# Turning the row maxima of an attention kernel by a DMA transpose instead of a TensorE product, and moving two staging slots

## The chip, the cores and the metric

The kernel runs on one core of one Trainium2 chip. The metric is the device time of one execution in microseconds. Before the change the median of three runs is 1665.59 us (1664.72 to 1666.26).

## The reference

One transformer block on a sequence of 2048 rows of width 512 (float32), with a modulation that a vector `c` sets:

```python
mod = (_silu(c) @ w_mod).reshape(c.shape[0], 6, 1, -1)
sa, ca, ga, sb, cb, gb = (mod[:, 0], ..., mod[:, 5])
h = _layernorm(x) * (1 + ca) + sa
x = x + ga * _A_ref(h, A_wq, A_wk, A_wv, A_wo)
h = _layernorm(x) * (1 + cb) + sb
x = x + gb * _B_ref(h, B_w_gate, B_w_up, B_w_down)
```

`_A_ref` is attention with 32 query heads of width 16 that share one key and one value head. `_B_ref` is a gated layer without a nonlinearity, `((h @ w_gate) * (h @ w_up)) @ w_down`, with 1792 inner columns. What matters here is the softmax over 2048 keys, `softmax(q k^T / 4)`, for each head and each query row.

## The kernel before

**Units.** The attention is done in 32 units. A unit `u` is 256 query rows (`ST`) of 8 heads, held as two halves `a`, each of four heads in pairs. Its queries lie in one of three buffers, `sst[u % 3]`, with the head's numbers on partitions 0 to 47 and 64 to 111. For a unit the kernel needs the row maximum of each of its 2048 (head, row) pairs before it may take exponentials. So there is a **maximum pass** over the scores, one unit ahead, and then the pass proper:

- `max_mm` (the product is L601) multiplies 128 query rows with 512 keys, and VectorE reduces the 128x512 product to one column of `mpart` (L605). Four such pairs stand in each turn of the main loop.
- When all of a unit's parts are there, `max_fin` (L622) reduces `mpart` to `mm`, 128 partitions x 16 columns: the query row lies on the partition, the half and head on the column.
- `max_rows` turns `mm`, since the pass proper wants the maxima as two further rows of the queries' buffer, partitions 48, 49 (and 112, 113): then one product yields the score minus its row's maximum. The maximum is held as a sum of two float16 numbers.
- `qk_exp` makes scores with the keys on partitions (L657 and L659, 50 rows deep: 48 and the two rows of maxima), and ScalarE takes the exponential into a tile `P` (L661).
- `pv` (L670) multiplies `P` with the values, eight products in a group, one turn later.

**The main loop.** `attend(u, kt)` writes two turns at a time, 16 turns to a unit, by a fixed pattern of score products, maximum products and "side" products (L511). The side products are the query projection in the first units, and then the output projection and the gated layer of rows that are finished. The pool of PSUM banks is a queue of eight; a tile that is "held" keeps its bank until it is given back. The kernel is under a manual schedule: what stands in an engine's queue, and in what order, is the order in which this code records it.

**Posts and timers.** `drain_posts()` runs at the start and in the middle of each turn and records what was put off: functions in `posts`, and those that `after(delay, f)` set for that many calls later.

**Turning the maxima before.** When a unit's last part is recorded, `max_rows(u)` gives two functions. The first (`f`, run by `late_max()` one step of the maximum pass later) holds a PSUM bank and lets TensorE multiply `mm` with the identity (L629, `mxt`). The second (`g`, at the next `drain_posts()`) lets ScalarE write the high half from PSUM to float16, scaled by 1/32 (L634, `mt`), lets VectorE write the rest (L635), and issues from SyncE one DMA of 2 x 8 x 128 numbers for each half into the two rows of `sst[u % 3]` (L639).

**The work that the SyncE queue carries.** Every DMA of the main loop is issued by SyncE (SP) in the order of recording: reloading queries (`load_q`, L566), saving and reloading a unit's outputs and their sums (L679, L686, L690, L695, L700), input rows and results (L733, L866), and the weights that come late (L937).

**Staging the late weights.** `stage(n)` loads one slice of a weight (448 or 512 columns of float32) into the next of the six slots of `SLOTS`, round and round. The slots are pieces of one large buffer, `kwb`, 14 slots long. While column norms are formed, the sums of squares lie in the same buffer: `ssqs[0]` from slot 4 on, 1792 columns (to the middle of slot 7), `ssqs[1]` the same length from slot 8 on. GpSimd squares a slice in its slot (L944) and adds it to those sums (L946). Slots 6 and 7 are thus used both for slices and for part of `ssqs[0]`.

Of the kernel before, what the change touches and what calls it, by code (L numbers as in the profile page):

```python
# [13 lines left out]
F32 = mybir.dt.float32  # L14
F16 = mybir.dt.float16
# [16 lines left out]
SQ_GAP = 2.6  # L32
LAG = 2
ROW_LAG = 4
SLOTS = (0, 1, 2, 3, 6, 7)
SUM_GAP = 4.0
SUM_LAG = 3
SPLIT_GAP = 2.5
# [25 lines left out]
def adaln_mqa_glu_kernel(ctx: ExitStack, tc: tile.TileContext, x_in, wq_in, wk_in, wv_in, wo_in,  # L64
# [159 lines left out]
    kwb = big.tile([128, 2 * FT * D], F16, name="kwb", tag="wd")  # L224
    hfs = kwb[:, 0:2 * NHF * BT].bitcast(F32).rearrange("p (n t) -> p n t", n=NHF)
    ssqs = [kwb[:, 2 * n * BT:2 * n * BT + 2 * F].bitcast(F32) for n in (KC, 2 * KC)]
    kng = kwb[:, 2 * NHF * BT:2 * NHF * BT + BT]

    def hf(b, k):
# [390 lines left out]
    def max_fin(u):  # L620
        mms[u] = work.tile([128, 2, 8], F32, name="mm")
        nc.vector.tensor_reduce(mms[u], mparts[u], axis=AX.X, op=OP.max)  # L622

    def max_rows(u):
        def f():
            mms[u, "b"] = ps_hold("mxt")
            p = mms[u, "b"][0:16, 0:128]
            mms[u, "p"] = p
            nc.tensor.transpose(p, mms[u].rearrange("p a c -> p (a c)"), ident)  # L629

        def g():
            p = mms[u, "p"]
            mt = [work.tile([16, 128], F16, name=f"mt{hl}") for hl in range(2)]
            nc.scalar.activation(mt[0], p, AF.Copy, scale=1.0 / 32.0)  # L634
            nc.vector.scalar_tensor_tensor(mt[1], p, 1.0 / 32.0, mt[0], op0=OP.mult, op1=OP.subtract)  # L635
            ps_give(mms[u, "b"])
            s = sst[u % 3]
            for hl in range(2):
                nc.sync.dma_start(s[48 + hl:113 + hl:64].rearrange("p c q n -> p (c q n)"), mt[hl])  # L639
        return [(100, f, g)]  # L640

    pvb = {}
    ptl = {}
# [249 lines left out]
    def late_weights():  # L893
# [37 lines left out]
        def stage(n):  # L931
            if "d" in W:
                t = work.tile([128, D], F32, name="wsl", tag="xl", bufs=3)
            else:
                t = hfs[:, SLOTS[taken[0] % len(SLOTS)], :]
                taken[0] += 1
            nc.sync.dma_start(t[:, :sl[n][3]], sl[n][2])  # L937
            st[n] = t
# [174 lines left out]

    wlist, dlist, mod_rows = late_weights()
    NSTEP = 32
    later = {}
    mstep = [0, 0]

    def drain_posts():
# [8 lines left out]
    def max_half(a):  # L1128
        n = mstep[a]
        mstep[a] += 1  # L1130
        if n >= len(flat):
            return
        u, i, last, ops = flat[n]
        max_parts(u)
        for kind, p, t, kc in ops[a]:
            max_mm(u, a, (kind, p, t, kc))
        if mstep[1 - a] <= n:
            return
        u, i, last, ops = flat[n]
        if 0 < u < NU - 1 and i == QPRE:  # L1140
            load_q(u + 1)
        if i == 12:
            max_parts(u + 1)
        if last:
            max_fin(u)
            (_, f, g), = max_rows(u)
            later[min(mstep) + 1] = (f, g)

    def late_max():
        for at in [m for m in later if m <= min(mstep)]:  # L1150
            f, g = later.pop(at)
            f()
            posts.append(g)
            return True
        return False

# [25 lines left out]
    qs = deque(q_proj(b, ch) for b in range(NB) for ch in ((2, 3, 0, 1) if b == 0 else range(KC)))  # L1184
    for n in range(LEAD):
        drain_posts()
        late_max()
        for _ in range(1 if n >= PAIRED else 2 - 2 * (n % 2)):
            max_half(0)
            max_half(1)  # L1190
# [27 lines left out]
    def attend(u, kt):  # L1218
# [10 lines left out]
        def end_turn(kt):  # L1229
# [7 lines left out]
            if v >= 0:  # L1237
                pv(*divmod(v, KT))
                if v % KT == KT - 1:
                    ends.append(lambda: pv_out(u - 1))  # L1240
            if not late_max() and turns and all(q.ended() for q in qs):
                _, f, post = turns.popleft()
                f()
                posts.append(post)
            hooks(u, 2 * kt + 1)

        for turn in range(2):
# [4 lines left out]
            for j, (what, a) in enumerate(order):  # L1252
                if j == len(order) // 2:
                    drain_posts()
                    if style is not NO_SIDE:
                        late_max()
                    hooks(u, 2 * (kt + turn))
                a = a if style is NO_SIDE else a ^ turn
                if what == "m" and mstep[a] >= len(flat) and style is MANY:
# [117 lines left out]
```

## Time and profile before

| what | us |
|---|---|
| median of three runs | 1665.59 |
| span of the profiled execution (first to last instruction) | 1663.8 |
| PE busy in it | 1643.3 |
| DVE busy | 1402.3 |
| ACT busy | 1234.8 |
| POOL busy | 523.5 |

The profiled execution's span leaves out what lies before the first and behind the last instruction; against the median of the runs that is 1.8 us. The profile calls TensorE's products PE and its weight loads PEld, VectorE DVE, ScalarE ACT, GpSimd POOL and the issuing of SyncE's DMAs SPq. In a timeline the columns are start (us), duration (us), engine, line, operation, output<-inputs, shapes, how many instructions the row joins, and in brackets the idle time of the engine before it with what ended it. In a group the numbers behind the bar are the busy time in us and the mean ns of one. Until 76 us the inputs are prepared; then unit 0 begins, and a unit takes some 41 to 49 us. The last unit's scores begin at 1505 us, and from 1551 us only the gated layer of the last rows is left.

### The profile page before, as it was taken

What the parts mean: (1) busy time and instruction counts of PE and PEld (TensorE: products, weight loads), DVE (VectorE), ACT (ScalarE), POOL (GpSimd) and SP (SyncE); (2) the same over time, 40 slices, a digit from 0 to 9 for tenths busy, and PEclk for the clock granted to TensorE, in tenths of its full rate; (3) what the DMA queues carried; (4) which work ended last, traced back from release to release, by engine and by line L of the source; (5) the groups of instructions that cost most, each with busy time, mean ns of one, the idle gap of its engine ahead of it and who ended that gap; (6) DMA issues with size and microseconds to landing.
All of it is one profiled execution on the core that took longest, in us unless ns stands there. A gap on an engine that the chain in (4) does not pass through costs nothing.

```text
span 1663.8 us, 39821 instructions
## 1 busy us (share of the span) xinstructions
PE 1643.3 (99%) x15677; PEld 747.1 (45%) x15677; DVE 1402.3 (84%) x2434; ACT 1234.8 (74%) x2389; POOL 523.5 (31%) x833
## 2 busy tenths in 40 slices
PE   8899999999999999999999999999999999999999
PEld 4333333355533554335543355434545345454776
DVE  7999999998998999899998999999998999980211
ACT  5688888888777877777877787777878777877300
POOL 4857537864841111301112011300113001210322
PEclk9999999999999999999999999999999999999999
DMA  6313313342210001000000000000000000000100
GB/s 237 108 59 100 95 43 120 96 129 80 77 51 24 18 12 32 19 32 20 20 26 23 25 13 24 26 25 26 20 29 15 26 22 20 26 14 21 33 13 14
DMA packets 66024, 75.39 MB, mean 45 GB/s; under 512 B 17702, under 2 KB 46634, under 8 KB 65836
## 3 DMA queue, kind: packets, MB, share of 16 engines
q1 hardware_dynamic: 63724, 72.26, 13.7%
q8 instruction: 123, 2.02, 0.5%
q10 hardware_dynamic: 2112, 0.59, 0.1%
q14 instruction: 65, 0.53, 0.1%
HBM read 55.51 MB, written 17.04 MB: 44 GB/s over the span
## 4 chain that ended last, share of the span: by engine, by line
PE 93%; ACT 2%; DVE 2%; DMA 1%; issue 1%; POOL 0%; SPq 0%; ACTq 0%; DVEq 0%
PE side L511 41%; PE pv L670 30%; PE mx L601 8%; PE sc L659 8%; PE sc L657 3%; ACT P L661 2%; DVE mpart L605 1%; DMA xbig<-in_A_x_dram 1%; PE mx L805 1%; PE mxt L629 0%; ACT hf L813 0%; PE sc L601 0%; DVE bs L248 0%; DMA kwb<-in_B_w_down_dram 0%; DMA wkv<-in_A_wv_dram 0%
## 5 line engine op out<-in xcount | busy, mean ns | idle before, releaser
L605 DVE TENSOR_REDUCE mpart<-mx 128x1 f32<-128x512 f32 x2016 | 1274.1, 684 | 104.0 <-PE mx L601 95.7
L661 ACT ACTIVATE P<-sc 128x512 f32<-128x512 f32 x2048 | 1094.8, 598 | 274.2 <-PE sc L659 226.9
L601 PE MATMUL mx<-kst,sst 48*128 48x512 f16 x2032 | 631.5, 377 | 3.8 <-ACT P L661 1.7
L659 PE MATMUL sc<-sst,kst 50*128 50x512 f16 x1792 | 597.5, 379 | 0.6 <-ACT P L661 0.3
L670 PE MATMUL pv<-P,vst 128*32 128x512 f32 x4096 | 545.3, 605 | 0.7
L511 PE MATMUL side<-h2T,wg 64*128 64x256 f16 (+1 forms) x2396 | 540.8, 271 | 0.1
L511 PE MATMUL side<-h2T,wu 64*128 64x256 f16 (+1 forms) x2396 | 538.7, 270 | 0.0
L511 PEld LDWEIGHTS <-wg 64*128 64x128 f16 (+1 forms) x2396 | 226.0, 94 | 230.5 <-ACT P L661 194.0
L511 PE MATMUL side<-wd,glu 64*128 64x512 f16 (+1 forms) x1172 | 272.8, 378 | 0.2 <-ACT P L661 0.2
L850 POOL TENSOR_SCALAR glu<-gf 128x256 f16<-128x256 f32 x112 | 45.8, 409 | 671.3 <-DVE gf L849 583.9
L511 PEld LDWEIGHTS <-wu 64*128 64x128 f16 (+1 forms) x2396 | 226.4, 94 | 43.0 <-issue 7.8
L601 PEld LDWEIGHTS <-sst 48*128 48x128 f16 x2064 | 189.9, 94 | 34.2 <-issue 17.4
L659 PEld LDWEIGHTS <-kst 50*128 50x128 f16 x1792 | 162.9, 94 | 63.0 <-issue 50.3
L511 PEld LDWEIGHTS <-glu 64*128 64x128 f16 (+1 forms) x1172 | 98.5, 94 | 192.4 <-ACT P L661 85.9
L670 PEld LDWEIGHTS pv<-P,vst 128*32 128x32 f32 x4096 | 80.7, 108 | 160.9 <-issue 150.1
L849 DVE TENSOR_TENSOR gf<-side,g 128x256 f32<-128x256 f32 x112 | 46.7, 418 | 79.8 <-ACT g L847 77.7
L657 PE MATMUL sc<-sst,kst 50*128 50x256 f16 x512 | 96.9, 268 | 0.1
L511 PE MATMUL side<-h,wq 64*128 64x512 f16 (+1 forms) x372 | 95.0, 376 | 0.4 <-ACT P L661 0.4
L847 ACT ACTIVATE g<-side 128x256 f32<-128x256 f32 x112 | 42.3, 379 | 65.6 <-PE side L511 65.3
L511 PE MATMUL side<-wo,och 64*128 64x512 f16 (+1 forms) x360 | 86.3, 377 | 0.0
L851 POOL TENSOR_TENSOR glu<-gf,glu 128x256 f16<-128x256 f32 x112 | 75.3, 673 | 9.3
L706 POOL TENSOR_TENSOR oc<-oc,rr 128x256 f32<-128x256 f32 x31 | 22.7, 731 | 146.6 <-DMA rr<-ri 100.4
(233 smaller groups left out, 865.4 us busy)
## 6 DMA issues: line engine op xcount, KB each, us to landing
pd<-ev SPq DMA_DIRECT2D x32, 256.0 KB
kwb<-in_B_w_gate_dram SPq DMA_DIRECT2D x32, 224.0 KB
kwb<-in_B_w_up_dram SPq DMA_DIRECT2D x32, 224.0 KB
sst<-qd SPq DMA_DIRECT2D x180, 32.0 KB
qd<-q SPq DMA_DIRECT2D x16, 256.0 KB
oc<-pd SPq DMA_DIRECT2D x64, 64.0 KB
rr<-ri SPq DMA_DIRECT2D x64, 64.0 KB
x<-in_A_x_dram SPq DMA_DIRECT2D x14, 256.0 KB
```

Source lines behind the costliest of these rows:

```text
L511: return nc.tensor.matmul(self.p[:, c * w:(c + 1) * w], left[rows], right[rows], start=start and c == 0, stop=stop and c == len(terms) - 1)
L601: nc.tensor.matmul(m, s[64 * a:64 * a + 48, t // 2, p, t % 2 * 128:(t % 2 + 1) * 128], w[64 * a:64 * a + 48, :], start=(i == 0), stop=(i = ...
L605: nc.vector.tensor_reduce(part, m, axis=AX.X, op=OP.max)
L657: nc.tensor.matmul(t[:, c * ST:(c + 1) * ST], keys, s[64 * a:64 * a + 50, c, p, :], start=True, stop=True)
L659: nc.tensor.matmul(t.rearrange("k (c n) -> k c n", c=2), keys, s[64 * a:64 * a + 50, :, p, :], start=True, stop=True)
L661: ex = nc.scalar.activation(ptl[u, kt, p, a], t, AF.Exp)
L670: nc.tensor.matmul(pvb[u][32 * j:32 * j + 32, :], vst[:, kt, :], ptl[u, kt, p, a], start=(kt == 0), stop=(kt == KT - 1))
L706: eng.tensor_tensor(o, o, st["r"], op=OP.mult)
L847: nc.scalar.activation(g, p[:, 0:ST], AF.Copy, scale=2.0 ** -45)
L849: nc.vector.tensor_tensor(gf, p[:, ST:2 * ST], g, op=OP.mult)
L850: nc.gpsimd.tensor_scalar(glu()[:, 0, f, :], gf, 1.0, 0.0, op0=OP.mult, op1=OP.add)
L851: nc.gpsimd.tensor_tensor(glu()[:, 1, f, :], gf, glu()[:, 0, f, :], op=OP.subtract)
```

## The change

`max_rows` now works on `mm` as it lies. VectorE writes `mm / 32` in float16 into the first 16 columns of a 128x128 float16 tile `mtc` (L632 of the changed kernel) and the rest into the next 16 (L633); the other columns are zeros, which GpSimd writes once at the start. There are two such tiles, used in turn. One `drain_posts()` later, SyncE issues a DMA with `transpose=True` of the whole 128x128 tile into `mtT`; two calls after that it issues the same two DMAs of rows as before, now from 16 partitions each of `mtT`. The product with the identity, its bank, ScalarE's copy, `late_max` and `later` are gone. Since `late_max()` no longer says that it did something, the piece of the main loop that takes work from `turns` no longer steps back for it.

Apart from that, the staging slots are now 0, 1, 2, 3, 12 and 13 of `kwb` instead of 0, 1, 2, 3, 6 and 7.

```diff
-SLOTS = (0, 1, 2, 3, 6, 7)
+ROWS_LAG = 2
+SLOTS = (0, 1, 2, 3, 12, 13)
...
+    stg = kwb.bitcast(F32).rearrange("p (n t) -> p n t", t=BT)
...
+    mtc = consts.tile([128, 2, 128], F16, name="mtc")
+    nc.gpsimd.memset(mtc, 0.0)
+    mtT = consts.tile([128, 2, 128], F16, name="mtT")
+
     def max_rows(u):
-        def f():
-            mms[u, "b"] = ps_hold("mxt")
-            p = mms[u, "b"][0:16, 0:128]
-            mms[u, "p"] = p
-            nc.tensor.transpose(p, mms[u].rearrange("p a c -> p (a c)"), ident)
-
-        def g():
-            p = mms[u, "p"]
-            mt = [work.tile([16, 128], F16, name=f"mt{hl}") for hl in range(2)]
-            nc.scalar.activation(mt[0], p, AF.Copy, scale=1.0 / 32.0)
-            nc.vector.scalar_tensor_tensor(mt[1], p, 1.0 / 32.0, mt[0], op0=OP.mult, op1=OP.subtract)
-            ps_give(mms[u, "b"])
+        m, c = mms[u].rearrange("p a c -> p (a c)"), mtc[:, u % 2, :]
+        nc.vector.tensor_scalar(c[:, 0:16], m, 1.0 / 32.0, None, op0=OP.mult)
+        nc.vector.scalar_tensor_tensor(c[:, 16:32], m, 1.0 / 32.0, c[:, 0:16], op0=OP.mult, op1=OP.subtract)
+        t = mtT[:, u % 2, :]
+
+        def rows():
             s = sst[u % 3]
             for hl in range(2):
-                nc.sync.dma_start(s[48 + hl:113 + hl:64].rearrange("p c q n -> p (c q n)"), mt[hl])
-        return [(100, f, g)]
+                nc.sync.dma_start(s[48 + hl:113 + hl:64].rearrange("p c q n -> p (c q n)"), t[16 * hl:16 * hl + 16, :])
+
+        after(1, lambda: nc.sync.dma_start(t, c, transpose=True))
+        after(1 + ROWS_LAG, rows)
...
-                t = hfs[:, SLOTS[taken[0] % len(SLOTS)], :]
+                t = stg[:, SLOTS[taken[0] % len(SLOTS)], :]
...
-            (_, f, g), = max_rows(u)
-            later[min(mstep) + 1] = (f, g)
+            max_rows(u)
...
-            if not late_max() and turns and all(q.ended() for q in qs):
+            if turns and all(q.ended() for q in qs):
```

The lines of the changed kernel carry numbers that are two higher around here (the product L601 is L603, the reduction L605 is L607).

On TensorE nothing moves but the 32 products with the identity, which go. The queue around the one of unit 3, with the unit's `sst_128` not yet in use (`sst_130` is unit 2's, whose scores are running, `sst_129` unit 4's, whose maxima are being formed). Before:

```order
L601 MATMUL mx<-kst,sst_129 128x512
L670 MATMUL pv<-P,vst 32x512 x4
L629 MATMUL mxt<-ident,mm 16x128
L659 LDWEIGHTS kst
L659 MATMUL sc<-sst_130,kst 128x512
L601 LDWEIGHTS sst_129
L601 MATMUL mx<-kst,sst_129 128x512
```

Now:

```order
L603 MATMUL mx<-kst,sst_129 128x512
L672 MATMUL pv<-P,vst 32x512 x4
L661 LDWEIGHTS kst
L661 MATMUL sc<-sst_130,kst 128x512
L603 LDWEIGHTS sst_129
L603 MATMUL mx<-kst,sst_129 128x512
```

The group of value products is now followed at once by the next turn's score product. In both kernels the first score product of the new unit stands behind the second group of value products after this place, in every unit from 1 on.

On VectorE the work on the maxima moves up to the reduction that makes them. Around unit 19 (`x_11103`, now `x_11064`, are result rows to which the gated layer is added). Before:

```order
L605 TENSOR_REDUCE mpart<-mx 128x1 x29
L622 TENSOR_REDUCE mm<-mpart 128x16
L605 TENSOR_REDUCE mpart<-mx 128x1 x2
L635 SCALAR_TENSOR_TENSOR mt_15689<-mxt,mt_15688 16x128
L605 TENSOR_REDUCE mpart<-mx 128x1 x4
L865 SCALAR_TENSOR_TENSOR x_11103<-side,sca,x_11103 128x512
```

Now:

```order
L607 TENSOR_REDUCE mpart<-mx 128x1 x29
L624 TENSOR_REDUCE mm<-mpart 128x16
L632 TENSOR_SCALAR mtc<-mm 128x16
L633 SCALAR_TENSOR_TENSOR mtc<-mm,mtc 128x16
L607 TENSOR_REDUCE mpart<-mx 128x1 x6
L867 SCALAR_TENSOR_TENSOR x_11064<-side,sca,x_11064 128x512
```

Two operations stand where one stood two reductions later.

On SyncE one DMA is added for each unit, and the two of rows can fall behind others. The queue at the same unit 19 (`sst_129` is its buffer, `out_dram` the store of those result rows, `pd` and `rc` the saved outputs of a unit and the reload of their sums). Before:

```order
L566 DMA sst_130<-qd_0_3023 16x4x256 x6
L639 DMA sst_129<-mt_15688 2x8x128
L639 DMA sst_129<-mt_15689 2x8x128
L866 DMA out_dram<-x_11103 128x512
L679 DMA pd_15891<-ev 128x512
L686 DMA rc<-pd_15891 128x1x16
```

Now:

```order
L568 DMA sst_130<-qd_0_3014 16x4x256 x6
L641 DMA_TRANSPOSE mtT<-mtc 128x128
L868 DMA out_dram<-x_11064 128x512
L639 DMA sst_129<-mtT 2x8x128 x2
L681 DMA pd_15834<-ev 128x512
L688 DMA rc<-pd_15834 128x1x16
```

The rows have fallen behind the store, which waits for VectorE's `x_11064`. It is the only unit where a store has come between. In units 1 to 3, 6 and 7 a load of weights stands between the transpose and the rows, in unit 5 a load of input rows and one of weights; in units 14, 23 and 28 a store that stood ahead of the rows now stands ahead of the transpose, in units 7 and 8 a load of weights that stood behind the rows does so too; in the other units the rows follow the transpose directly.

More of the change, by code (lines that the diff above doesn't have):

```diff
@@ L1115, in adaln_mqa_glu_kernel @@
     NSTEP = 32
-    later = {}
     mstep = [0, 0]
@@ L1145, in max_half @@
             max_fin(u)
-            (_, f, g), = max_rows(u)
-            later[min(mstep) + 1] = (f, g)
[L1149 to L1155, printed above, removed]
+            max_rows(u)
     fill = deque()
@@ L1186, in adaln_mqa_glu_kernel @@
         drain_posts()
-        late_max()
         for _ in range(1 if n >= PAIRED else 2 - 2 * (n % 2)):
@@ L1254, in attend @@
                     drain_posts()
-                    if style is not NO_SIDE:
-                        late_max()
                     hooks(u, 2 * (kt + turn))
```

## Prediction

> **What bounds the kernel now.** I read the page's first lines, then the chain of waits with its shares by line, then the removed tile, and then timelines around single units.
>
> ```profile
> PE 1643.3 (99%) x15677; PEld 747.1 (45%) x15677; DVE 1402.3 (84%) x2434; ACT 1234.8 (74%) x2389; POOL 523.5 (31%) x833
> PE 93%; ACT 2%; DVE 2%; DMA 1%; issue 1%; POOL 0%; SPq 0%; ACTq 0%; DVEq 0%
> by line: PE side L511 41.2%; PE pv L670 29.9%; PE mx L601 8.5%; PE sc L659 8.2%; PE sc L657 2.8%; ACT P L661 1.7%; DVE mpart L605 1.0%; DMA xbig<-in_A_x_dram 0.6%; PE mx L805 0.6%; issue 0.5%; PE mxt L629 0.4%; ACT hf L813 0.4%; PE sc L601
> ```
>
> TensorE is busy for 99% of the span and is 93% of the chain. So what is taken out of its queue shortens the run, unless something else is late in the same turn. The chain holds the products to be removed with 0.4%, which is 0.004 x 1663.8 = 6.7 us.
>
> ```profile
> L629 PE MATMUL mxt<-ident,mm x32: 269/277/278, 68.3 to 1499.5; 128*16 128x128 f32 x32
> L634 ACT ACTIVATE mt<-mxt x32: 250/267/268, 68.6 to 1499.9; 16x128 f16<-16x128 f32 x32
> L635 DVE SCALAR_TENSOR_TENSOR mt<-mxt,mt x32: 267/278/279, 70.5 to 1500.2; 16x128 f16<-16x128 f32 x32
> ```
>
> Products are pipelined, so 277 ns is not yet what one costs. TensorE around unit 27 shows it:
>
> ```profile
> 1308.84 1.06 PE L670 MATMUL pv<-P,vst 128*32 128x512 f32 x8
> 1311.67 1.07 PE L670 MATMUL pv<-P,vst 128*32 128x512 f32 x8
> 1312.67 0.28 PE L629 MATMUL mxt<-ident,mm 128*16 128x128 f32 x1
> 1312.88 0.39 PE L511 MATMUL side<-wd,glu 64*128 64x512 f16 x1
> ...
> 1317.65 1.07 PE L670 MATMUL pv<-P,vst 128*32 128x512 f32 x8
> 1318.65 0.39 PE L511 MATMUL side<-wd,glu 64*128 64x512 f16 x1
> 1318.66 0.39 PE L659 MATMUL sc<-sst,kst 50*128 50x512 f16 x1
> ```
>
> A plain turn is 1311.67 - 1308.84 = 2.83 us. Behind a group of value products the next product starts 1.00 us after the group (1317.65 to 1318.65); with the transpose it starts 1.21 us after it (1311.67 to 1312.88). One transpose costs the queue 0.21 us. The last row is the first score product of unit 27: the second group after the transpose ends there, and this product reads the rows of maxima. That is the deadline of the new route.
>
> **What goes.** TensorE: 32 x 0.21 = 6.7 us, on the bound engine, the same as the chain's share. ScalarE: 32 x 0.267 = 8.5 us, which I cost at nothing, since ScalarE is busy 74%. Their waits go too:
>
> ```profile
> ACT mt L634 <- PE mxt L629: 15.0, 29, 2.9
> DVE mt L635 <- ACT mt L634: 2.6, 5, 1.2
> L605 DVE TENSOR_REDUCE mpart<-mx 128x1 f32<-128x512 f32 x2016 | 1274.1, 684 | 104.0 <-PE mx L601 95.7
> ```
>
> ScalarE stood 15.0 us for the transposes and VectorE 2.6 us for ScalarE. Mostly these hid in time that the engines had spare anyway (VectorE waits 95.7 us for TensorE's products), so I book nothing for them; the bound on the other side is the product's whole 0.277 us and VectorE's waits, 32 x 0.277 + 2.6 = 11.5 us. The freed bank is booked at nothing as well.
>
> **What VectorE gets.** One operation of 278 ns goes, two of 128 x 16 come. Small ones cost it this:
>
> ```profile
> 63.99 0.22 DVE L404 TENSOR_REDUCE evs<-ident 128x1 f32<-128x64 f32 x1
> 64.12 0.15 DVE L405 RECIPROCAL evt<-kb 128x1 f32<-128x1 f32 x1
> 64.19 0.68 DVE L610 CUSTOM_DVE_ANT_0 rel<-mx,rel 128x512 f32<-128x512 f32 x1
> 1313.28 0.28 DVE L635 SCALAR_TENSOR_TENSOR mt<-mxt,mt 16x128 f16<-16x128 f32 x1
> 1313.53 2.56 DVE L605 TENSOR_REDUCE mpart<-mx 128x1 f32<-128x512 f32 x4
> ```
>
> From start to start they take 0.07 to 0.13 us, so two make 0.14 to 0.26 where the old one took 0.25 (1313.28 to 1313.53). Zero, with bounds of -0.11 and +0.01 us a unit.
>
> **The new route and its deadline.** VectorE is in order and writes the parts directly behind `mm`. SyncE then issues the transpose, waits until it has landed, and issues the rows. Behind the waiting SyncE stand saves and reloads that begin 10 us later. No row shows a transposing DMA; call its time from issue to landing T. The other pieces have rows, here for unit 3, the tightest:
>
> ```profile
> 194.70 0.22 DVE L622 TENSOR_REDUCE mm<-mpart 128x16 f32<-128x64 f32 x1
> 194.84 1.28 DVE L605 TENSOR_REDUCE mpart<-mx 128x1 f32<-128x512 f32 x2
> 196.03 1.20 SPq L639 DMA_DIRECT2D sst<-mt  x2
> 199.77 1.06 PE L670 MATMUL pv<-P,vst 128*32 128x512 f32 x8
> 200.77 0.39 PE L659 MATMUL sc<-sst,kst 50*128 50x512 f16 x1
> 217.78 0.33 SPq L695 DMA_DIRECT2D ri<-rc  x1
> 219.25 1.10 SPq L700 DMA_DIRECT2D rr<-ri  x2
> 250.02 0.34 SPq L679 DMA_DIRECT2D pd<-ev  x1
> 252.02 0.57 SPq L686 DMA_DIRECT2D rc<-pd  x1
> ```
>
> After `mm` starts: 0.14 to the next operation, 0.13 for the first new one, 0.2 until the second has written, 0.03 to SyncE: the transpose is issued at 0.5 us. A DMA that waits for another's landing starts 1.47 us after the other was issued when that moves 8 KB (L695 to L700), and 2.00 us when it moves 256 KB (L679 to L686). The two rows: the second is issued some 0.65 us after the first (half of 1.20), and lands 1.45 us on: 2.1. Unit 3: issue at 195.20, deadline 200.77 less the 0.21 that goes = 200.56; T may be 200.56 - 195.20 - 2.14 = 3.2 us. A unit like 27 (`mm` starts at 1311.88, read beside the rows above):
>
> ```profile
> 1311.88 0.22 DVE L622 TENSOR_REDUCE mm<-mpart 128x16 f32<-128x64 f32 x1
> ```
>
> 1318.45 - 1312.38 - 2.14 = 3.9 us. T has a lower bound of 1.47 us, the smaller handover. From above: moved number by number it would be 16384 pieces, 1024 for each of 16 engines. The page's smallest packets are those of q10:
>
> ```profile
> q10 hardware_dynamic: 2112, 0.59, 0.1%
> ```
>
> 0.001 x 16 x 1663.8 us / 2112 = 13 ns each, so 13 + 1.5 = 14 us. I take T = 2.0 us: 32 KB lie between the two handovers, and the tile is 128 rows of 256 bytes, like the row DMAs' pieces. At 2.0 there is no wait in nearly all units.
>
> The Trainium skill speaks against the change here: "VectorE: DVE Perf Modes", section "The three transpose paths", gives 390 ns for TensorE and 1309 ns for the DMA crossbar on a 128x128 tile, and its rules say to use TensorE where a destination in PSUM will do. The trace has 277 ns for the former (16 columns, float32); for the latter no run here shows a figure yet. By the Trainium skill's figure alone T would be an estimated 1.3 us, and the sum would be the same as at 2.0, since neither stalls a plain unit; its rule ranks by latency, while this kernel pays for TensorE's time.
>
>
> **Where the queue is worse.** Rows that fall behind others: loads of weights and inputs are issued while the transpose flies, free. In unit 19 a store that waits for VectorE's result comes between, and in unit 14 one stands ahead of the transpose:
>
> ```profile
> 942.10 0.74 DVE L865 SCALAR_TENSOR_TENSOR x<-side,sca,x 128x512 f32<-128x512 f32 x1
> 942.87 0.36 SPq L866 DMA_DIRECT2D out_dram<-x  x1
> 944.80 0.39 PE L659 MATMUL sc<-sst,kst 50*128 50x512 f16 x1
> 707.17 0.36 SPq L866 DMA_DIRECT2D out_dram<-x  x1
> 712.12 0.39 PE L659 MATMUL sc<-sst,kst 50*128 50x512 f16 x1
> ```
>
> Unit 19: rows start at 942.87 + 0.41 = 943.28 and land at 945.38; deadline 944.80 - 0.21 = 944.59: 0.8 us of stall. Unit 14: VectorE's two operations now precede the store's, so the transpose goes out at about 707.8; at T = 2.0 the rows land at 711.9, just at the deadline of 711.91. Sum of stalls: 0.8 us.
>
> **The rest.** GpSimd clears `mtc` early, in a gap of 1.72 us:
>
> ```profile
> 31.01 0.99 POOL L438 TENSOR_SCALAR kwb<-kwb,fwd 128x512 f32<-128x512 f32 x1 [1.72 <-PE part L279]
> PEld mx L956 <- POOL kwb L946: 2.5, 1, 2.5
> ```
>
> Nothing. The new slots take the staged slices away from GpSimd's sums of squares. TensorE waited for those sums once, 2.5 us, behind a queue of other work on GpSimd that stays. I take zero, bounds -2.5 and +1.
>
> **Sum.** -6.7 + 0.8 = -5.9: the profiled span goes from 1663.8 to 1657.9. The median of the runs stands 1.8 us above that span; 1665.6 - 5.9 = 1659.7.
>
> **Rivals.** What a measurement of this kernel can tell from no change is about 0.2%, 3.3 us: 1662.3 and 1668.9 are the borders.
>
> 1. *Rows too late* (slower): the transpose outlasts the slack, and TensorE stands before each unit. It starts at T = 3.2 in units 1 to 3 and 3.9 in the others, and eats the gain at about T = 4.1. At T = 5, 28 x 1.1 + 3 x 1.8 + about 2 (units 14, 19) = 38 us of stalls, so 1665.6 - 6.7 + 38 = 1697. At the upper bound of 14 us, in which the change would not do what it says since nothing is turned on the fly, 31 x 10.1 - 6.7 = +306 us. For it: no row bounds T closely. Against it: the two handovers above are 1.47 and 2.00 us, and T would have to be twice the longer. Chance 0.15. The skill's preference for TensorE, above, would be right in this case.
> 2. *Two full handovers in series* (about the same): each waiting DMA takes the longer handover, and turning costs the shorter one on top. T is then 2.00 + 1.47 = 3.47, and the rows land 0.65 + 2.00 = 2.65 us after their issue. Slack in units like 27: 1318.45 - 1312.38 - 2.69 = 3.38, a stall of 0.09 in each of some 26, 2.3 us; units 1 to 3 about 0.7 each; unit 19 0.8 + 0.55 = 1.35; unit 14 707.8 + 3.47 + 2.69 - 711.91 = 2.05. Together 7.8 against 6.7 saved: 1666.7. For it: the landing of the rows themselves has no row of its own. Against it: the 2.00 belongs to 256 KB. Chance 0.10. The Trainium skill, "DMA: Bandwidth & Descriptors", section "Latency and other measured facts", puts a DMA's fixed cost at about 2 us, where L695 to L700 shows 1.47; by it and the 1309 ns an estimated T of 3.3 us would end near here.
> 3. *Gain lost beside TensorE* (about the same): VectorE's turn becomes the limit. Four reductions take 2.56 us (the row x4 above); with `mm` (0.14) and the two operations (up to 0.26) that is 2.96 against the plain turn of 2.83. If VectorE sets each such turn, 0.13 x 32 = 4.2 us of the gain go: 1663.9. Against it: VectorE idles 104 us before these reductions and can catch up over neighbouring turns through eight banks. Chance 0.08.
> 4. *More gained*: the waits count too, 11.5 us and up to 2.5 from the slots: about 1655. Chance 0.04.
>
> The forecast has 0.63. The range leaves out most of rival 1, and the outer part of rival 4: 1655.8 to 1670. Faster by over 0.2%: 0.61 of the forecast and 0.04 of rival 4, 0.65. Same: 0.02 of the forecast, 0.10 of rival 2 and 0.08 of rival 3, 0.20. Slower: 0.15 of rival 1.
>
> **What would show it.** PE's count falls by 32, its busy time by about 6 to 9 us; behind value products the next product starts 1.00 us later in every turn. SyncE's issue of rows follows that of the transpose by T, 2.0 us, in units without a store between. Waits of TensorE for `sst<-mtT` appear in unit 19 alone, 0.8 us. The forecast is wrong if that wait comes at each unit's first score product (rivals 1 and 2), or if turns with `mm` stay at 3.05 us with VectorE as the releaser (rival 3).

## The result and the profile after

The changed kernel takes 1676.68 us (median of 4 runs, 1674.92 to 1679.48) against 1665.92 us for the kernel before on the same chip (1664.72 to 1666.4). The ratio is 1.0068, 95% interval 1.0056 to 1.0080: slower, by some 10.8 us, where 1659.7 was forecast. The profiled execution has a span of 1673.1 us against 1663.8, so its traces explain 9.3 us.

The page's first line, the chain by engine and by line, and the group of VectorE's reductions, in the changed kernel:

```profile
PE 1647.0 (98%) x15645; PEld 743.5 (44%) x15645; DVE 1409.8 (84%) x2466; ACT 1227.3 (73%) x2357; POOL 523.7 (31%) x834
PE 89%; DVE 6%; ACT 2%; DMA 2%; issue 1%; SPq 0%; POOL 0%; ACTq 0%
PE side L513 39%; PE pv L672 28%; PE mx L603 8%; PE sc L661 8%; DVE mpart L607 4%; PE sc L659 3%; ACT P L663 2%; DMA xbig<-in_A_x_dram 1%; PE mx L807 1%; DVE mtc L632 0%; PE sc L603 0%; DVE mtc L633 0%; DVE bs L250 0%; DMA pd<-ev 0%; DVE mm L624 0%
L607 DVE TENSOR_REDUCE mpart<-mx 128x1 f32<-128x512 f32 x2016 | 1270.7, 684 | 105.7 <-PE mx L603 95.3
```

The 32 products are gone (15677 to 15645). TensorE's busy time nevertheless rose, by 3.7 us, where a fall of 6 to 9 was forecast; the profile models the ends of products, so this figure does not tell work from waiting. What moved is the chain: VectorE's share went from 2% to 6%, and that of its reductions from 1.0% to 4%. VectorE's own idle time hardly changed (104.0 to 105.7 us), so the average says nothing; the place does.

The new pieces, as tiles (min/median/max ns):

```profile
L632 DVE TENSOR_SCALAR mtc<-mm x32: 174/175/1031, 68.1 to 1508.4; 128x16 f16<-128x16 f32 x32
L633 DVE SCALAR_TENSOR_TENSOR mtc<-mm,mtc x32: 174/176/1015, 68.4 to 1508.6; 128x16 f16<-128x16 f32 x32
L641 SPq DMA_TRANSPOSE mtT<-mtc x32: 1131/1132/1191, 68.6 to 1508.9; - x32
```

The medians of VectorE's two operations are small, but the largest are six times as long. The transfer that the forecast worried about most behaves: SyncE needs 1.13 us to issue it, and the rows follow it 2.25 to 2.35 us later in most units, here in unit 23:

```profile
1133.96 1.13 SPq L641 DMA_TRANSPOSE mtT<-mtc  x1
1136.24 1.16 SPq L639 DMA_DIRECT2D sst<-mtT  x2
```

TensorE waited for the rows only in units 14 and 19, 0.9 us in all (the turns in which they arrive are 0.57 and 0.94 us longer than before):

```profile
PE sc L661 <- DMA sst<-mtT: 0.9, 2, 0.7
```

The loss builds up by units. The start of `mm`, against the kernel before, is 0.1 us earlier in unit 3, 3.0 us later in unit 4, 4.8 in unit 8, 8.0 in unit 20, 9.4 in unit 31, and the end is 9.3 us later. So it has two parts: large steps, mostly in early units, and small ones later. It lies in the turn in which the maxima are finished: summed over units 1 to 31, the two turns from `mm` on take 9.5 us more than before. The turns with late rows in units 14 and 19 add 1.5 us, and other turns give 1.7 back.

What TensorE waited for there is VectorE's reductions. These are its longer waits for them (0.15 us or more) in the main loop, the first row before, the others after; all of the latter lie in the two turns from `mm` on, in units 3 to 7, 9, 19, 22, 26 and 30:

```profile
PE mx L601 <- DVE mpart L605: 0.6, 2, 0.4
```

```profile
PE mx L603 <- DVE mpart L607: 2.7, 5, 1.5
PE sc L661 <- DVE mpart L607: 1.3, 4, 0.5
PE side L513 <- DVE mpart L607: 1.1, 5, 0.2
```

**The small steps, unit 24.** TensorE before, then VectorE and TensorE after:

```profile
1170.46 1.06 PE L670 MATMUL pv<-P,vst 128*32 128x512 f32 x8
1171.46 0.28 PE L629 MATMUL mxt<-ident,mm 128*16 128x128 f32 x1
1173.52 1.07 PE L670 MATMUL pv<-P,vst 128*32 128x512 f32 x8
```

```profile
1179.20 0.22 DVE L624 TENSOR_REDUCE mm<-mpart 128x16 f32<-128x64 f32 x1
1179.45 0.17 DVE L632 TENSOR_SCALAR mtc<-mm 128x16 f16<-128x16 f32 x1
1179.66 0.18 DVE L633 SCALAR_TENSOR_TENSOR mtc<-mm,mtc 128x16 f16<-128x16 f32 x1
1179.75 1.28 DVE L607 TENSOR_REDUCE mpart<-mx 128x1 f32<-128x512 f32 x2
```

```profile
1179.09 1.07 PE L672 MATMUL pv<-P,vst 128*32 128x512 f32 x8
...
1180.75 0.27 PE L513 MATMUL side<-h2T,wg 64*128 64x256 f16 x1
1181.09 0.37 PE L661 MATMUL sc<-sst,kst 50*128 50x512 f16 x1
...
1182.32 1.06 PE L672 MATMUL pv<-P,vst 128*32 128x512 f32 x8
```

The turn was 1173.52 - 1170.46 = 3.06 us and is 1182.32 - 1179.09 = 3.23 us. (In units 23 and 25 it is 3.05 and 3.02 us, about what it was with the product: there only the gain is lost.) From `mm` to the next reduction VectorE now needs 0.55 us instead of 0.14: each of the two operations starts 0.03 to 0.04 us after the end of the one whose result it reads. The pair of reductions behind them ends at 1179.75 + 1.28 = 1181.03, and 0.06 us later, at 1181.09, a score product starts, 0.34 us after the product ahead of it instead of the usual 0.1. A score product reads nothing of these reductions, nor does a side product, and yet the waits above have rows for both, in other units. What they can take from them is a PSUM bank: score and maximum products share the queue of eight.

**The large steps, unit 3.** VectorE, then GpSimd, then TensorE:

```profile
194.56 0.22 DVE L624 TENSOR_REDUCE mm<-mpart 128x16 f32<-128x64 f32 x1
194.82 1.03 DVE L632 TENSOR_SCALAR mtc<-mm 128x16 f16<-128x16 f32 x1
195.88 0.85 DVE L633 SCALAR_TENSOR_TENSOR mtc<-mm,mtc 128x16 f16<-128x16 f32 x1
196.66 1.28 DVE L607 TENSOR_REDUCE mpart<-mx 128x1 f32<-128x512 f32 x2
```

```profile
194.68 1.14 POOL L948 TENSOR_TENSOR kwb<-kwb 128x448 f32<-128x448 f32 x1
195.77 0.93 POOL L946 TENSOR_TENSOR kwb<-kwb 128x448 f32<-128x448 f32 x1
```

```profile
197.39 0.37 PE L603 MATMUL mx<-kst,sst 48*128 48x512 f16 x1 [1.50 <-DVE mpart L607]
```

L632 ends at 195.85, GpSimd's first operation at 195.82; L633 ends at 196.73, GpSimd's second at 196.70. Each of VectorE's operations of 0.17 us ends just when GpSimd's has ended, and TensorE then stands 1.50 us for a reduction. `mm` itself is not stretched beside GpSimd (0.22 us everywhere). The stretching shows in units 3, 5, 6, 7, 9, 18, 22, 26 and 30 (and by 0.05 us in unit 0), and adds 6.9 us to VectorE's operations over the run.

### The profile page after: what moved, and what is told of

Same layout as the page of the kernel before. It is cut to its first block, busy times and chain, and to the rows that moved or that the text cites. A ratio compares the mean times of both kernels' runs of the same rounds, so it can differ in the third digit from the quotient of the medians.

```text
span 1673.1 us, 39691 instructions
## 1 busy us (share of the span) xinstructions
PE 1647.0 (98%) x15645; PEld 743.5 (44%) x15645; DVE 1409.8 (84%) x2466; ACT 1227.3 (73%) x2357; POOL 523.7 (31%) x834
## 4 chain that ended last, share of the span: by engine, by line
PE 89%; DVE 6%; ACT 2%; DMA 2%; issue 1%; SPq 0%; POOL 0%; ACTq 0%
PE side L513 39%; PE pv L672 28%; PE mx L603 8%; PE sc L661 8%; DVE mpart L607 4%; PE sc L659 3%; ACT P L663 2%; DMA xbig<-in_A_x_dram 1%; PE mx L807 1%; DVE mtc L632 0%; PE sc L603 0%; DVE mtc L633 0%; DVE bs L250 0%; DMA pd<-ev 0%; DVE mm L624 0%
## 5 line engine op out<-in xcount | busy, mean ns | idle before, releaser
L607 DVE TENSOR_REDUCE mpart<-mx 128x1 f32<-128x512 f32 x2016 | 1270.7, 684 | 105.7 <-PE mx L603 95.3
L603 PE MATMUL mx<-kst,sst 48*128 48x512 f16 x2032 | 632.4, 377 | 6.0 <-DVE mpart L607 2.7
L603 PEld LDWEIGHTS <-sst 48*128 48x128 f16 x2064 | 189.3, 94 | 38.9 <-issue 21.8
```

The lines of the kernel that those rows point to most:

```text
L603: nc.tensor.matmul(m, s[64 * a:64 * a + 48, t // 2, p, t % 2 * 128:(t % 2 + 1) * 128], w[64 * a:64 * a + 48, :], start=(i == 0), stop=(i = ...
L607: nc.vector.tensor_reduce(part, m, axis=AX.X, op=OP.max)
```

## The experiments

Theory A: VectorE's time directly behind the maxima sets those turns, by its two operations and their stretching beside GpSimd. B: it is the staging slots. C: it is the added transfer in the queue of SyncE. All ratios are against the kernel before, with 95% intervals.

**The two halves of the change.** Slots alone are three lines of the diff (`SLOTS`, `stg`, `stage`) put into the kernel before; the other run is the changed kernel with

```diff
-SLOTS = (0, 1, 2, 3, 12, 13)
+SLOTS = (0, 1, 2, 3, 6, 7)
```

> The kernel before with the new staging slots alone. Theory A (VectorE sets the length of the turns in which the maxima are finished, and its two new operations are what is paid): the slots play no part, within 1.5 us of the kernel before, 1664.5 to 1667.5. Theory B (the slots are what is paid: loads and GpSimd's squares fall differently in the first 430 us): 1670 to 1676, and the loss at unit 3 (a wait of TensorE of about 1.5 us near 197 us) is there too. Theory C (the added DMA and the SyncE queue are what is paid): as before, 1666.

> The changed kernel with the old staging slots. Theory A: as the changed kernel, 1674 to 1679. Theory B: 1659 to 1667, the removed products show as a gain. Theory C: as the changed kernel.

Slots alone: 1666.36 us, 1.0004 (0.9995 to 1.0013). Turning alone: 1676.60, 1.0070 (1.0057 to 1.0082). B falls.

**The split on GpSimd.**

```diff
-        nc.vector.tensor_scalar(c[:, 0:16], m, 1.0 / 32.0, None, op0=OP.mult)
-        nc.vector.scalar_tensor_tensor(c[:, 16:32], m, 1.0 / 32.0, c[:, 0:16], op0=OP.mult, op1=OP.subtract)
+        nc.gpsimd.tensor_scalar(m, m, 1.0 / 32.0, 0.0, op0=OP.mult, op1=OP.add)
+        nc.gpsimd.tensor_scalar(c[:, 0:16], m, 1.0, 0.0, op0=OP.mult, op1=OP.add)
+        nc.gpsimd.tensor_tensor(c[:, 16:32], m, c[:, 0:16], op=OP.subtract)
```

> The changed kernel with the split of the maxima done by GpSimd (three operations) instead of VectorE. Theory A: VectorE loses 0.42 us and all stretched operations in each of these turns, TensorE's 0.21 us come through: about 1660 (1657 to 1664), with turns of some 2.84 to 2.9 us where the maxima are finished late in the run; a late row at a unit where GpSimd is busy may cost back 1 to 2 us. Theory B and theory C: 1673 or more, since slots, DMAs and queue are those of the changed kernel.

Measured: 1686.34, 1.0129 (1.0115 to 1.0143), so the expectation failed. TensorE's wait for the rows says why:

```profile
PE sc L662 <- DMA sst<-mtT: 16.3, 9, 4.8
```

GpSimd's queue stood behind other work, so the rows came late, up to 4.8 us. Between those units TensorE won back what the product had cost: from unit 11 to unit 18 its lag shrank from 23.95 to 22.18 us, 0.25 a unit.

**The maxima in a PSUM bank**, where VectorE reads them from another memory:

```diff
-        mms[u] = work.tile([128, 2, 8], F32, name="mm")
+        mms[u] = ps_hold("mm", (128, 2, 8))
...
+        ps_give(mms[u])
```

> The changed kernel with mm kept in a PSUM bank, so that neither of VectorE's two operations has two SBUF inputs or a single SBUF source. Theory A with both terms (0.17 us more VectorE work in each unit, 5.3 us, and operations stretched beside GpSimd's, 7.2 us in the profile of the changed kernel): the stretched ones go, each operation takes some 0.2 us, and the time is 1668 to 1671. Theory A with the stretching alone: about 1660 to 1664. Theory A with the load alone, or theory B or C: 1674 or more.

Measured: 1672.39, 1.0041 (1.0027 to 1.0054). The stretching is gone altogether, with GpSimd's work where it was:

```profile
L632 DVE TENSOR_SCALAR mtc<-mm x32: 173/174/176, 68.1 to 1504.6; 128x16 f16<-128x16 f32 x32
L633 DVE SCALAR_TENSOR_TENSOR mtc<-mm,mtc x32: 173/174/175, 68.3 to 1504.8; 128x16 f16<-128x16 f32 x32
```

Some 4.3 us of the 10.8 come back; 1668 to 1671 had been expected. The lag is 2.0 us in unit 9 and 5.6 in unit 31, but what is left is not paid behind the maxima: the two turns from `mm` on, 9.5 us longer than before in the changed kernel, are now 3.3 us shorter (units 1 to 31). It is the turn ahead of `mm` that has grown, by 0.06 to 0.46 us in 30 of these 31 units and by 7.0 us in all. In every kernel here with the maxima in SBUF that sum is 0.0. VectorE gains time in the longer turn, so the 12.8 us that the turns behind `mm` lost are not the stretching alone.

**Counting VectorE's operations and TensorE's products.** One after the other: the product made twice, the two operations made twice, only one of them, the low half left out of the kernel before, and both things at once, the kernel before with the two operations added.

```diff
             nc.tensor.transpose(p, mms[u].rearrange("p a c -> p (a c)"), ident)
+            nc.tensor.transpose(p, mms[u].rearrange("p a c -> p (a c)"), ident)
```

> The kernel before, with each of its 32 products with the identity made twice in a row (the second overwrites the first with the same values). It measures what such a product costs the kernel before. If TensorE alone sets the length of those units, as the prediction had it, 32 more products of 0.21 us add 6.7 us: about 1672.6. If VectorE sets them in the turns where the maxima are finished (the present theory, in its strong form), TensorE has room there and it is under 1669; at no cost at all 1666.

```diff
+        nc.vector.tensor_scalar(c[:, 0:16], m, 1.0 / 32.0, None, op0=OP.mult)
+        nc.vector.scalar_tensor_tensor(c[:, 16:32], m, 1.0 / 32.0, c[:, 0:16], op0=OP.mult, op1=OP.subtract)
```

> The changed kernel, with VectorE's two small operations done twice over. Theory A (VectorE's time in these turns counts in full): 31 units by 0.42 us, the step of the two as they ran, is 13 us, and the second pair is stretched beside GpSimd as the first was, up to 4 us more: 1688 to 1695. If the loss comes from the queue of the added transfers or from where they land (theory C), or from anything but VectorE: 1676.7 as it is.

```diff
-        nc.vector.scalar_tensor_tensor(c[:, 16:32], m, 1.0 / 32.0, c[:, 0:16], op0=OP.mult, op1=OP.subtract)
```

> The changed kernel with the second of the two small operations left out, so that the low half of each maximum stays zero and the maxima are less exact. Theory A: 31 by 0.21 us and about half of the stretching beside GpSimd (some 2 to 3 us) come back, so 1667 to 1670, near the kernel before. Theory C: the transfers are all still there, so 1676.

```diff
-            mt = [work.tile([16, 128], F16, name=f"mt{hl}") for hl in range(2)]
+            mt = [work.tile([16, 128], F16, name="mt0"), mt1]
...
-            nc.vector.scalar_tensor_tensor(mt[1], p, 1.0 / 32.0, mt[0], op0=OP.mult, op1=OP.subtract)
```

> The kernel before with its own VectorE operation on the low half left out (a constant tile of zeros goes in its place), so that VectorE has 0.25 us less in a unit, some turns later than the maxima, and the product with the identity stays. If VectorE's load already sets the pace of these units in the kernel before, up to 32 by 0.25 us come back: 1658 to 1662. If TensorE sets it there, nothing: 1666.

```diff
         nc.vector.tensor_reduce(mms[u], mparts[u], axis=AX.X, op=OP.max)
+        m, c = mms[u].rearrange("p a c -> p (a c)"), work.tile([128, 32], F16, name="mtd")
+        nc.vector.tensor_scalar(c[:, 0:16], m, 1.0 / 32.0, None, op0=OP.mult)
+        nc.vector.scalar_tensor_tensor(c[:, 16:32], m, 1.0 / 32.0, c[:, 0:16], op0=OP.mult, op1=OP.subtract)
```

> The kernel before with the changed kernel's two VectorE operations added behind the maxima, into a tile that nobody reads; the product with the identity and everything behind it stay. If the slower of TensorE and VectorE sets the turn (the present theory), the 0.21 us of the product lie beside VectorE's work as soon as the two operations are there, and the time is that of the changed kernel: 1675 to 1678. If TensorE's product and VectorE's operations add up: 1666 + 9.3 + 6.6 = 1682 or more. If the loss is in the transfers: 1666.

| kernel | us | ratio (95%) |
|---|---|---|
| before, product twice | 1667.25 | 1.0009 (1.0000 to 1.0017) |
| after, two operations twice | 1694.20 | 1.0170 (1.0156 to 1.0184) |
| after, one operation | 1665.89 | 1.0004 (0.9995 to 1.0013) |
| before, low half left out | 1665.83 | 0.9999 (0.9990 to 1.0008) |
| before plus the two operations | 1681.51 | 1.0092 (1.0078 to 1.0106) |

The operations made twice and the product made twice came out where one of the expectations had them (1688 to 1695, and under 1669), the single operation 1 us under its 1667 to 1670. But the medians alone mislead: a product more seems to cost nearly nothing, as if TensorE did not count. So I took the length of the turn behind `mm` from each trace, from the start of one group of value products to the next. In us, with the first kernel of the last experiment below (its split on ScalarE, a half turn later) as the plain turn; the last column is the sum over units 8 to 31 (that turn and the one behind it) against the kernel before:

| kernel | unit 23 | unit 24 | unit 25 | units 8 to 31 |
|---|---|---|---|---|
| no product, nothing on VectorE | 2.84 | 2.85 | 2.85 | -4.9 |
| product (before) | 3.05 | 3.05 | 3.05 | 0 |
| product twice | 3.15 | 3.16 | 3.16 | +2.1 |
| one operation | 2.84 | 3.02 | 2.85 | -1.1 |
| two operations (after) | 3.05 | 3.23 | 3.02 | +3.6 |
| four operations | 3.47 | 3.65 | 3.44 | +14.0 |
| product and two operations | 3.27 | 3.42 | 3.24 | +8.0 |

Read down. The product costs 0.21 us in each unit, as forecast. Made twice, it costs 0.11 more, not 0.21:

```profile
1172.03 0.28 PE L629 MATMUL mxt<-ident,mm 128*16 128x128 f32 x1
1172.15 0.27 PE L630 MATMUL mxt<-ident,mm 128*16 128x128 f32 x1
```

and the 2.8 us that the turns from `mm` on take more (units 1 to 31) are partly given back in places that have nothing to do with it: a turn of unit 7 that took 4.00 us before, with a wait of 0.89 us for ScalarE, takes 2.85 there. Scattered waits come and go by such amounts, which is why the turns decide here and not a median that is 1 us off.

VectorE's first operation is free in two of the three units and costs 0.17 us in the third; the second costs 0.18 to 0.22 in all, and a second pair 0.42, its full step. So there is about 0.2 us of room behind `mm` in units 23 and 25 and less in unit 24, and from there on VectorE's time counts in full. And the product counts on top of it, 0.19 to 0.22 us: theory A in the form "the slower of the two engines sets the turn", on which the expectation of 1675 to 1678 for the last kernel rested, is wrong. Its rows in unit 24, VectorE and then TensorE, show how the two add up:

```profile
1184.93 1.28 DVE L605 TENSOR_REDUCE mpart<-mx 128x1 f32<-128x512 f32 x2
```

```profile
1185.26 0.28 PE L632 MATMUL mxt<-ident,mm 128*16 128x128 f32 x1
1185.92 0.27 PE L511 MATMUL side<-h2T,wg 64*128 64x256 f16 x1
1186.27 0.37 PE L662 MATMUL sc<-sst,kst 50*128 50x512 f16 x1
```

The score product starts 0.06 us after the end of the reductions again (1184.93 + 1.28 = 1186.21). But it is the second score product of the turn, where in the changed kernel it was the third: the product with the identity holds a bank of its own, so TensorE runs into the occupied bank one product earlier, and its 0.21 us are not hidden by the wait. The kernel with one operation shows the same contact a third time, reductions to 1172.40 and the score product at 1172.46. This reading by banks rests on three traces and on the waits above. The only runs in which the queue has a bank less at another place are the two that hold the maxima in one, and there the turn ahead of `mm` grows.

C falls with these runs too: the kernel with one operation has every added transfer and takes 1665.89, and so has one that takes 1662.96 (below). Leaving the transposing transfer itself out wasn't tried.

**Who else could split.** ScalarE writes the high half from the maxima as they lie and the low half stays zero; the same with VectorE's low half one reduction behind the maxima; and that with the low half two half turns later.

```diff
-        nc.vector.tensor_scalar(c[:, 0:16], m, 1.0 / 32.0, None, op0=OP.mult)
-        nc.vector.scalar_tensor_tensor(c[:, 16:32], m, 1.0 / 32.0, c[:, 0:16], op0=OP.mult, op1=OP.subtract)
+        nc.scalar.activation(c[:, 0:16], m, AF.Copy, scale=1.0 / 32.0)
```

> The changed kernel with the high half written by ScalarE from the maxima as they lie, and the low half left out (it stays zero, the maxima are less exact), so that VectorE has neither of the two operations and TensorE has no product. Theory (slower of the two engines): now TensorE's 0.207 us in 31 or 32 units show: 1666 - 6.6 + 0.9 for the rows that come late in two units = 1660. If the product was worth nothing, as the run with it made twice (+1.2 us) might be read: 1666.

```diff
-        after(1, lambda: nc.sync.dma_start(t, c, transpose=True))
+        def low():
+            nc.vector.scalar_tensor_tensor(c[:, 16:32], m, 1.0 / 32.0, c[:, 0:16], op0=OP.mult, op1=OP.subtract)
+            nc.sync.dma_start(t, c, transpose=True)
+
+        after(1, low)
```

> The changed kernel with the high half written by ScalarE and only the low half by VectorE, one reduction behind the maxima, as the kernel before has its own low half; nothing of the computation is left out. If VectorE has the 0.2 us to spare there, as the kernel before without its low half (no change) says: 1660. If it has no room once the product no longer makes the turn longer, it is as with one operation in a row: 1664 to 1667; and more if VectorE waits there for ScalarE.

```diff
-        after(1, low)
-        after(1 + ROWS_LAG, rows)
+        after(2, low)
+        after(3, rows)
```

> As the kernel with the high half on ScalarE, with the low half and the transfer behind it two half turns later, three reductions behind the maxima instead of one. If what VectorE lacks is room in the turn of the maxima: the plain turns behind it have up to 0.09 us to spare, so 1662 to 1665, and better than the kernel with the low half one reduction behind. If the rows then come too late for TensorE, it is slower, by the wait for them times the units in which it shows, 0.5 to 1 us by 32: over 1675.

Measured: 1665.45, 0.9998 (0.9989 to 1.0006); 1670.78, 1.0031 (1.0020 to 1.0041); 1685.00, 1.0113 (1.0097 to 1.0129). The first missed its 1660 by 5 us. Its turns are 3.05, 2.97 and 3.03 us in units 23 to 25, though neither the product nor VectorE's operations are there; ScalarE stood for the maxima, where its exponentials should have been:

```profile
ACT mtc L632 <- DVE mm L624: 11.3, 27, 2.7
```

In units 18, 22, 26 and 30 ScalarE did not wait, and there the turns are only 0.05 us longer than plain ones. The low half one reduction further on adds nothing to these turns (their sums over units 8 to 31 are -1.7 us without and -1.6 with it), but the transfer behind it is later, and the rows are late in four units; still later, they are late in 19. The turns in which they arrive are then 4.5 and 18.9 us longer than before in all. So the one came out over the 1664 to 1667 that had been expected of VectorE's room, and the other in the case that was named for late rows (over 1675). TensorE's waits, first in the one, then in the other kernel:

```profile
PE sc L664 <- DMA sst<-mtT: 3.2, 4, 1.0
```

```profile
PE sc L664 <- DMA sst<-mtT: 11.4, 19, 1.6
```

**ScalarE later, and one operation without stretching.** These two were run to find out whether the product's 6.6 us can be had at all. In the first, ScalarE's operation stands a half turn later, without a low half (VectorE's two operations are out, as above); the second is the changed kernel with the maxima in a PSUM bank and no low half.

```diff
-        after(1, lambda: nc.sync.dma_start(t, c, transpose=True))
+        def high():
+            nc.scalar.activation(c[:, 0:16], m, AF.Copy, scale=1.0 / 32.0)
+            nc.sync.dma_start(t, c, transpose=True)
+
+        after(1, high)
```

> As the kernel with the high half on ScalarE and no low half (the low half stays zero), but ScalarE's operation and the transfer behind it a half turn later, one exponential further on, where ScalarE finds the maxima done. If the missing 5 us there were ScalarE's wait of 0.25 us for the maxima in each unit, with its exponentials and TensorE behind it, the turns are as long as plain ones, and the time is 1660, or up to 1664 where the later transfer brings the rows too late in a few units. If taking the product out gives nothing in the total, whoever splits the maxima: 1665 to 1666 again.

> The changed kernel with the maxima in a PSUM bank and the low half left out (it stays zero): VectorE has one operation of 0.21 us in a unit, and no operation of GpSimd stretches it. Theory (VectorE's time in these turns counts once it exceeds some 0.2 us, the product's time does come back): under the same kernel with the maxima in SBUF (1665.9) by the stretching, 2 to 4 us: 1662 to 1664. If the stretching is hidden when only one operation is there: 1666.

The first: 1662.96, 0.9985 (0.9976 to 0.9994), as expected, and the only kernel here that beats both. In unit 24, its turn and the score product that waited in the changed kernel (VectorE's reductions end at 1169.01):

```profile
1167.73 1.28 DVE L607 TENSOR_REDUCE mpart<-mx 128x1 f32<-128x512 f32 x2
```

```profile
1167.48 1.07 PE L674 MATMUL pv<-P,vst 128*32 128x512 f32 x8
...
1169.15 0.37 PE L663 MATMUL sc<-sst,kst 50*128 50x512 f16 x1
...
1170.33 1.06 PE L674 MATMUL pv<-P,vst 128*32 128x512 f32 x8
```

Its waits for the rows:

```profile
PE sc L663 <- DMA sst<-mtT: 1.3, 2, 0.6
```

The turn is 2.85 us, that of a plain one, and the score product starts 0.14 us after the reductions' end, without a wait. Over units 8 to 31 the product's 0.20 us a unit come back in full (-4.9 us). Late rows take 1.3 us of waiting back in units 19 and 28, and in units 0 to 4 ScalarE still waits for the maxima, 5.0 us in all, so that the turns of units 1 to 5 win nothing. It leaves the low half out; that this is no gain by itself the run of the kernel before without it says (1665.83).

The second: 1666.98, 1.0007 (0.9998 to 1.0016), where 1662 to 1664 was expected. The trace has both signs in it: against the kernel with one operation and the maxima in SBUF it is 2.2 us ahead at unit 8, after the units with most of the stretching, and only 0.3 us at unit 31: it loses some 0.08 us a unit. Behind the maxima it loses nothing: over units 8 to 31 these turns are 5.0 us shorter than before, like the -4.9 of the kernel with nothing on VectorE. It loses in the turn ahead of `mm`, again 7.0 us over units 1 to 31. Ahead of unit 24's maxima:

```profile
1166.31 1.07 PE L672 MATMUL pv<-P,vst 128*32 128x512 f32 x8
...
1169.04 0.27 PE L513 MATMUL side<-h2T,wg 64*128 64x256 f16 x1
1169.37 0.27 PE L659 MATMUL sc<-sst,kst 50*128 50x256 f16 x1
...
1169.67 1.06 PE L672 MATMUL pv<-P,vst 128*32 128x512 f32 x8
```

This turn is 3.36 us, 0.45 more than before, and a score product stands 0.33 us behind the product ahead of it. The two kernels with one operation differ only in where `mm` lies, so the bank that the maxima hold is what this turn pays. Which product waits for which bank was not followed.

## Why the prediction was wrong

**The product, -6.7 us: right in the price of one.** 0.21 us a unit were taken out, and over units 8 to 31 the runs find 0.20 (before against the kernel with nothing in the turn) and 0.18 (the changed kernel against the kernel before with the two operations added). Over units 1 to 31 the turns are 5.7 us shorter with the split on GpSimd, and 4.5 with ScalarE's late operation.

**What VectorE gets, zero with bounds of -0.11 and +0.01 us a unit: this step failed,** in three ways.

- The size. This is the term that was mis-sized. The two operations were priced at 0.07 to 0.13 us each from rows whose neighbours don't depend on each other. These do: `mm`, the high half and the low half each read what the one before has written, and from `mm` to the next reduction it takes 0.55 us instead of 0.14, 0.42 for the two.
- The credit. The old operation's 0.25 us were set against them. It stood later, where VectorE's time costs nothing (leaving it out: 0.9999). What is saved there does not help behind `mm`.
- The company. Beside an operation of GpSimd the two took up to 1.03 us. The forecast moved an operation's input from PSUM to SBUF and did not ask who else is there.

Together, against the kernel with the split on GpSimd, which has neither the product nor these operations in its turns, the two operations cost 15.2 us in the turns of units 1 to 31: 6.8 in units 1 to 7 (0.98 each, where most of the stretching is) and 8.4 in units 8 to 31 (0.35 each). Its turns are 5.7 us shorter than before's. 15.2 - 5.7 = 9.5, and the span grew by 9.3.

**Rival 3 had the mechanism's engine, not its price.** It had VectorE's turn become the limit, at 0.13 us a unit, and gave it 0.08, since "VectorE idles 104 us before these reductions and can catch up over neighbouring turns through eight banks". Both halves of that sentence were read from an average. In the plain turn of unit 24 the reductions end 0.14 us before the bank is used again; that is the room there, not 104 us. The signs that were named for this rival came: turns with `mm` of 3.05 us in unit 23 and 3.02 in unit 25, and VectorE's reductions as releaser wherever a wait is long enough to be listed. But the gain was not merely lost beside TensorE, as that rival had it: 5.7 us came, and more than twice as much was taken away.

**The new route: right.** T was taken as 2.0 us and is 2.25 to 2.35 in most units; for the forecast stall of 0.8 us in unit 19 the waits are 0.67 there and 0.20 in unit 14 (1.5 us by the length of these turns). The time from the rows' issue to their landing stands once as 2.1 and once as 2.14 us, and half of 1.20 is 0.60, not 0.65; neither moves the sum. Rivals 1 and 2 are refuted. The Trainium skill's 1309 ns for the crossbar ("VectorE: DVE Perf Modes", section "The three transpose paths") is not what a waiting queue sees: the trace has 1.13 us for the issue alone, and 2.25 us or more until the rows are issued.

**ScalarE's waits and the slots at nothing: right** (slots 1.0004).

A rule that bore on this and was overlooked: the Trainium skill, "SBUF — State Buffer", section "SBUF: two separate sides", says that VectorE and GpSimd share a pair of ports by an exclusive lock for a whole instruction, where VectorE's operation has two inputs in SBUF or runs in a mode that uses both ports. The trace agrees: the stretched operations end 0.03 us after GpSimd's (195.85 against 195.82), the reduction `mm`, with one input, is never stretched (0.22 us), and with the maxima in PSUM neither operation is (176 ns at most). That L632, with its one input, runs in such a mode no row shows.

## What to carry to other kernels

Price an operation where it will stand in its engine's queue: what waits behind it, how soon the bank or buffer that the next one frees is wanted, and who shares its memory port at that time; an engine's idle total says nothing about that place. A chain of small operations that read each other costs its full length, not the step of independent ones. And when work leaves the bound engine, look whether it comes back as a wait of that engine: turn by turn in two traces, since medians of a microsecond hide it.

## What the runs showed of the hardware that was not expected

- VectorE's operations of 128 x 16 elements with inputs in SBUF (0.17 us) are held until a GpSimd operation that began before them ends, up to 1.03 us; from PSUM they took 173 to 176 ns in all 32 units, whatever GpSimd did.
- A transposing DMA of one 128x128 float16 tile takes SyncE's queue 1.13 us to issue, and a DMA that reads its result is issued 2.22 us after it at the earliest in these runs.
- The same product with the identity a second time in a row cost TensorE 0.11 to 0.12 us, where the first cost 0.21.
- An activation on ScalarE that waits 0.27 us for VectorE behind the maxima lengthened TensorE's turns by 0.12 to 0.22 us in units 23 to 25, with ScalarE busy 74%; where it did not wait, by 0.05.
- Maxima held in one of the eight PSUM banks, instead of in SBUF, lengthened the turn ahead of them by up to 0.46 us, 7.0 us in all, in both kernels that do it.
